# Tile 2's gate and value products as block products, with a new order of the steps around it

## The chip, the cores and the metric

The kernel runs on 1 core of a Trainium2 chip. Its engines are TensorE (PE), VectorE (DVE), ScalarE (ACT), GpSimd (POOL) and SyncE (SP), which here issues nearly all DMAs. The metric is the time of one execution in microseconds on the device; the median of several executions is what is compared.

## The reference

Causal attention with a window of 64 keys (8 batches, 8 heads, 576 positions, 64 per head), and behind it a gated layer on its 4608 tokens:

```python
scores = where(mask, q @ k.T / sqrt(64), -1e9)          # mask: 0 <= i - j < 64
x = softmax(scores) @ v                                 # 4608 tokens x 512
xn = x / sqrt(mean(x * x) + 1e-6) * rms_g
g = xn @ w_gate                                         # 512 x 1536
out = (g * sigmoid(g) * (xn @ w_val)) @ w_out           # 1536 x 512
```

All inputs and outputs are float32.

## The kernel before

The tokens are worked through in nine tiles of 512 (`t` = 0 to 8). The inner width of 1536 is cut into six chunks of 256 (`c`). For each tile the kernel first makes gate and value of all chunks ("gate and value stage"), then the product with `w_out` ("out stage"). Operands are split into a high and a low half in float16, and a product is the sum of three: high by high, high by low, low by high (`three`, L1534).

There are two ways for gate and value. Tiles 0 to `FIRST7` - 1 = 2 use `expert_in` (L1578): for each chunk and each half of it a product `pg` (gate) and one `pv` (value), each of 12 matmuls with 512 columns, in one of three PSUM banks of the pool `ps_mo`; ScalarE takes tanh of `pg` into `th`, VectorE multiplies `th` by `pg` and then by `pv`, and ScalarE and GpSimd split the result into the halves of `h`. Tiles from `FIRST7` on use `expert_in_7` (L1733): weights and tokens are cut into two by two blocks, and seven block products replace eight. A block product (`product`, L1717) has 12 matmuls with 256 columns, gate and value side by side in one bank `bk`. ScalarE copies three partial banks per chunk to SBUF (`s1`, `p5`, `u2`), VectorE adds them to the next ones, and the gates work on 256 columns at a time. Tiles from `FIRSTO` = 3 on also make their out stage by block products; tiles 0 to 2 use `expert_out` with the whole `h` (`chunk_out`).

The block products need seven left operands per chunk: three blocks of the weights and four sums of blocks. `prepare(c, step)` (L1628) makes them from the halves that lie in `wt0` to `wt11`: VectorE adds halves to whole blocks (`sum0`, `sum1`, `blk`), adds these, ScalarE casts to the high half of `hl`, VectorE subtracts for the low half, and SyncE writes both to DRAM (`sevens`). There are 50 such steps, `PREP` says between which points of time they fall. Time is counted in half steps, 32 to a tile: 24 in gate and value, 8 in out. `load_sevens` (L1705) later loads the operands, 256 KB each, into a ring of 15 places that are the high halves of `wt0` to `wt7`: so a place can be loaded when the last classic tile is through with that chunk's weights and `prepare` has read them.

The right operands of a tile in block form are made by `combine` (L1499): sums and differences of blocks of the tokens, split into halves. They lie in the tile's `xn`, in `wt18` or `wt19` by the parity of the tile (`operands`, L1489), and in `wt8` or, for the first such tile, in a small tile `t3`. Tile 1's first chunk of `h` lies in `wt18` (`HPLACE`, `h_tile`).

Between the products lies the attention of later batches, one visit for a pair of heads: TensorE makes scores and the product with the values; VectorE masks; ScalarE takes the exponential and scales; 13 copies of 32 rows exchange blocks of `pm` and VectorE turns them. `MOVE_ON` deals the copies out in turn: two for GpSimd, one for ScalarE.

Each engine works its instructions in order. That order is written out by hand: instructions are recorded, and the tables `ORDER` to `ORDER_3` say in which order they are emitted (a letter for the engine, the tile's name; `t` is the next TensorE step). `ORDER` holds all up to the end of tile 0's gate and value ("early list"); the others what follows.

The lines that matter most:

```python
FIRST7 = 3
PREP = ((27.5, 32, 9), (35, 88, 41))
for n, (c, p) in enumerate(SEVENS):
    x, y, w = banks[(c + parity(t)) % 2], banks[2], banks[5]
    acc = {1: x, 6: x, 7: x, 4: x, 2: y, 5: w, 3: w}[p]
    product(t, c, p, acc, p in (1, 2, 5))
```

Of the kernel before, what the change touches and what calls it, by code (L numbers as in the profile page):

```python
# [46 lines left out]
FIRST7 = 3  # L47
# [10 lines left out]
PREP = ((27.5, 32, 9), (35, 88, 41))  # L58
# [4 lines left out]
MOVE_ON = "gga"  # L63
SCALE = 0.5, 0.2
MOVE_BY = 0.8
# [126 lines left out]
t*39 s.pm_8 t*2 v.ssq_1 v.pm_8 s.pm_8 t v.ssq_1 t*2 s.pm_8 t*2 v.pm_8 t v.ssq_1 s.pm_8 t*4 v.pm_8 g.below t g.three_of  # L192
v.ssq_1 g.below t s.pm_8 v.pm_8 g.below*2 t v.ssq_1 g.below v.pm_8 g.below t s.pm_8 g.below v.ssq_1 t g.below v.pm_8
g.below t g.three_of v.ssq_1 g.three_of v.pm_8 s.pm_8 t g.three_of v.ssq_1 g.three_of t v.ssq_1 s.pm_8 t v.ssq_1 t
v.ssq_1 t s.pm_8 v.ssq_1 t*2 v.st_8 t v.ssq_1 t v.st_8 v.ssq_1 t s.pm_8*2 t s.pm_8 t s.pm_8 t s.pm_8 t s.pm_8 t s.pm_8
t s.pm_8 t s.pm_8 t*2 s.pm_8 g.pm_8 s.pm_8 g.pm_8*3
# [3 lines left out]
y.sevens3 v.sum1 y.sevens3 v.sum0 y.sevens3 v.sum1 v.blk_0_3 y.sevens3 v.sum1 y.sevens3 t*2 y.outs v.blk_0_3 t s.hl_0_2  # L200
t y.outs t s.pm_8 t y.outs s.pm_8 t*5 y.outs v.xb_1 t*2 y.outs g.pm_8 t v.xb_1 t s.xn_1 y.outs t*2 v.xb_1 y.sevens5
s.xn_1 t g.xn_1 t y.sevens0 t s.pm_8 v.xb_1 t s.xn_1 y.sevens5 t v.hl_0_2 t g.xn_1 y.sevens5 s.xn_1 t*2 y.sevens5
v.sum0 t*2 y.sevens5 t*3 y.sevens5 t g.xn_1 t y.sevens5 t v.xb_1 s.hl_0_4 t y.sevens0 v.xb_1 t v.xb_1 t s.xn_2
y.sevens5 v.xb_1 t s.xn_2 t s.xn_2 v.hl_0_4 g.xn_1 y.sevens5 t s.xn_2 t y.sevens5 v.sum1 t*3 y.sevens5 t*7 y.sevens0
# [307 lines left out]
def tile_window_attention_moe(  # L512
# [484 lines left out]
    def scores_of_pair(n, sc, first):  # L997
# [30 lines left out]
        for i, u in enumerate(order):  # L1028
            after(done + SCALE[0] + SCALE[1] * i, partial(even, u))

# [1134 lines left out]
```

## Time and profile before

| | us |
|---|---|
| median of 3 runs | 931.2 |
| lowest and highest | 930.34, 932.97 |
| the profiled execution | 933.73 |
| its span | 931.9 |

The span is what the hardware profiler saw of the profiled execution, from its first instruction to its last; its own time has 1.8 us more around it. In the views, `line` is that of a recording helper, so instructions are told apart by their tiles: `pg`, `pv`, `po` are banks of the classic products, `bk` banks of block products. The stages of this execution, by the first matmul of each: tile 0's out from 142.80 us, tile 1 from 175.93, its out from 249.71, tile 2 from 286.02, its out from 355.49, tile 3 from 390.94, its out from 452.3.

### The profile page before, as it was taken

How to read it: one execution, taken by the hardware profiler on the slowest of the kernel's cores; microseconds unless marked ns; L12 is line 12 of the kernel's file. 1: busy time of each engine (PE TensorE's matmuls, PEld its weight loads, DVE VectorE, ACT ScalarE, POOL GpSimd, SP SyncE). 2: the span in 40 equal slices, each digit the busy share in tenths (PEclk: the TensorE clock that was granted, in tenths of full speed). 3: DMA queues.
4: the chain of work that ended last, by engine and by line, in shares of the span. 5: the costliest groups of instructions: out<-in, count | busy, mean ns of one | idle time of the engine just before them, and what ended most of it. 6: DMA issues, size and time to landing. Idle time of an engine off the chain costs nothing.

```text
span 931.9 us, 23553 instructions
## 1 busy us (share of the span) xinstructions
PE 912.2 (98%) x8668; PEld 669.7 (72%) x8668; DVE 708.3 (76%) x1970; ACT 639.2 (69%) x1692; POOL 399.7 (43%) x555
## 2 busy tenths in 40 slices
PE   9799999999999999999999999999999999999998
PEld 6545544544444444588888888888888888888887
DVE  6799889676786898688868987888778767734760
ACT  7679987668646776599858886888598435623550
POOL 4355554545364563245444644455445322220330
PEclk9799999999999999999999999999999999999999
DMA  9775666653316744298868777777776667777613
GB/s 289 227 243 175 238 181 161 165 162 98 115 53 181 226 136 124 68 369 247 262 218 241 231 245 238 232 233 219 235 216 188 210 218 203 202 243 206 185 58 125
DMA packets 124772, 183.22 MB, mean 197 GB/s; under 512 B 30192, under 2 KB 59888, under 8 KB 124656
## 3 DMA queue, kind: packets, MB, share of 16 engines
q1 hardware_dynamic: 124080, 180.83, 64.0%
q8 instruction: 68, 1.11, 0.5%
q10 hardware_dynamic: 576, 0.88, 0.3%
q14 instruction: 48, 0.39, 0.1%
HBM read 155.72 MB, written 25.95 MB: 195 GB/s over the span
## 4 chain that ended last, share of the span: by engine, by line
PE 68%; DVE 12%; ACT 10%; DMA 5%; issue 3%; POOL 1%; SPq 1%; ACTq 0%; DVEq 0%; POOLq 0%
PE bk L574 48%; PE po L574 7%; ACT pm L574 6%; DMA kv<-kv 4%; PE pg L574 3%; PE xp L574 3%; DVE th L574 3%; PE pv L574 2%; PE sc L574 2%; DVE pm L574 2%; DVE sum L574 1%; POOL pm L574 1%; ACT th L574 1%; PE pw L574 1%; DVE hl L574 1%
## 5 line engine op out<-in xcount | busy, mean ns | idle before, releaser
L574 PEld LDWEIGHTS <-wt 128*128 128x128 f16 x3912 | 381.2, 98 | 140.6 <-issue 9.6
L574 PE MATMUL bk<-xn,wt 128*128 128x256 f16 x1728 | 208.3, 273 | 0.6 <-DMA wt<-sevens 0.4
L574 POOL TENSOR_TENSOR hw<-th,hw 128x256 f16<-128x256 f32 x72 | 68.0, 962 | 247.4 <-ACT hw L574 189.8
L574 PE MATMUL bk<-hw 128*128 128x256 f16 x1512 | 169.4, 273 | 0.6 <-ACT ot L574 0.6
L574 PEld LDWEIGHTS <-hw 128*128 128x128 f16 x1512 | 146.7, 98 | 18.7 <-issue 1.8
L574 ACT ACTIVATE pm<-pm,st 128x128 f32<-128x128 f32 (+1 forms) x432 | 149.3, 385 | 10.5 <-DVE st L574 10.3
L574 PE MATMUL bk<-wt,wt 128*128 128x256 f16 x1224 | 150.4, 273 | 2.0 <-ACT u L574 2.0
L574 POOL COPY pm<-pm 32x288 f32<-32x288 f32 (+1 forms) x218 | 107.3, 492 | 94.8 <-ACT pm L574 86.3
L574 PE MATMUL pg<-xn,wt 128*128 128x512 f16 x432 | 108.2, 380 | 0.4 <-DVE th L574 0.4
L574 PE MATMUL pv<-xn,wt 128*128 128x512 f16 x432 | 106.3, 380 | 1.0 <-DVE th L574 1.0
L574 PE MATMUL po<-wt,h 128*128 128x512 f16 x408 | 90.7, 379 | 0.0
L574 ACT ACTIVATE th<-bk,hsc 128x256 f32<-128x256 f32 x108 | 51.0, 472 | 37.9 <-PE bk L574 18.0
L574 PEld LDWEIGHTS <-h 128*128 128x128 f16 x408 | 39.2, 98 | 46.3 <-issue 0.5
L574 DVE SCALAR_TENSOR_TENSOR th<-th,bk 128x256 f32<-128x256 f32 x108 | 44.8, 415 | 27.5 <-ACT th L574 27.0
L574 POOL TENSOR_TENSOR xn<-xb,xn 128x448 f16<-128x448 f32 (+7 forms) x49 | 40.6, 848 | 40.3 <-ACT xn L574 39.8
L574 POOL TENSOR_TENSOR h<-th,h 128x512 f16<-128x512 f32 x30 | 38.7, 1292 | 39.8 <-ACT h L574 35.3
L574 DVE TENSOR_TENSOR bk<-bk,s 128x512 f32<-128x512 f32 x36 | 25.1, 697 | 31.9 <-PE bk L574 14.8
L574 PE MATMUL sc<-kv,q 64*64 64x128 f32 (+1 forms) x1056 | 47.7, 279 | 1.0 <-DVE ssq L574 0.7
L574 DVE SCALAR_TENSOR_TENSOR th<-bk,th 128x256 f32<-128x256 f32 x108 | 45.2, 418 | 2.1
L574 DVE STREAM_TRANSPOSE pm<-pm 128x512 f32<-128x512 f32 (+1 forms) x72 | 38.7, 556 | 10.1 <-POOL pm L574 9.8
L574 DVE CUSTOM_DVE_ANT_0 pm<-sc,blocked 128x128 f32<-128x128 f32 x192 | 44.2, 278 | 0.6 <-PE sc L574 0.6
L574 POOL TENSOR_TENSOR hw<-sb,hw 128x512 f16<-128x512 f32 x36 | 42.9, 1192 | 0.9 <-ACT hw L574 0.8
(184 smaller groups left out, 1495.1 us busy)
## 6 DMA issues: line engine op xcount, KB each, us to landing
wt<-sevens SPq DMA_DIRECT2D x252, 256.0 KB, 3.1
hw<-outs SPq DMA_DIRECT2D x84, 384.0 KB, 5.3
kv<-kv SPq DMA_DIRECT2D x28, 608.0 KB, 4.9
q<-q SPq DMA_DIRECT2D x29, 288.0 KB, 4.6
kv<-kv SPq DMA_DIRECT2D x65, 128.0 KB, 5.5
st<-w_gate SPq DMA_DIRECT2D x6, 1024.0 KB, 9.2
st<-w_val SPq DMA_DIRECT2D x6, 1024.0 KB, 6.8
st_o<-w_out SPq DMA_DIRECT2D x6, 1024.0 KB, 5.1
```

Source lines behind the costliest of these rows:

```text
L574: steps[next(tensor) if name == "t" else name].popleft()()
```

## The change

`FIRST7` becomes 2, so tile 2's gate and value are made by 42 block products; its out stage stays classic. All preparation of the blocks has to be made before it: the second stretch of `PREP` ends at 63 half steps, in tile 1's out stage, and not at 88. Tile 2's right operands now lie in `wt18`, so tile 1's first chunk of `h` lies in `wt19`. `MOVE_ON` deals the copies of a visit out one by one to GpSimd and ScalarE. `SCALE_ON` brings a way to scale weights on other engines, but "aaa" leaves all of it on ScalarE. `ORDER_0`, `ORDER_1` and `ORDER_3` are written anew; `ORDER` is the same.

```diff
-FIRST7 = 3
+FIRST7 = 2
...
-PREP = ((27.5, 32, 9), (35, 88, 41))
+PREP = ((27.5, 32, 9), (32.5, 63, 41))
...
-MOVE_ON = "gga"
+MOVE_ON = "ga"
 SCALE = 0.5, 0.2
+SCALE_ON = "aaa"
...
 ORDER_1 = """
-y.q_10 y.sevens0*12 y.sevens1*5 y.q_11 y.sevens1*7 y.sevens2 y.kv_10*3 y.sevens2*11 y.sevens4 y.sevens3*7 v.sum0
...
         for i, u in enumerate(order):
-            after(done + SCALE[0] + SCALE[1] * i, partial(even, u))
+            part = SCALE_ON[slot(u) // 4]
+            if part == "a":
+                after(done + SCALE[0] + SCALE[1] * i, partial(even, u))
+            elif u == 0:
+                after(done + SCALE[0], partial(even_first, engine_of(part)))
+            elif slot(u) % 4 == 0:
+                after(done + SCALE[0] + SCALE[1] * i, partial(even_four, engine_of(part), slot(u)))
...
-    HPLACE = "8fffff"
+    HPLACE = "9fffff"
```

`even_four` and `even_first`, which the diff also brings, are called for no letter of "aaa".

VectorE's order in tile 1's gate and value stage, from the last step on `th_1_2` on (first the tile, then the half of a chunk, 0 to 11). Before:

```order
L574 SCALAR_TENSOR_TENSOR th_1_2_2221<-pv_1_2_2222,th_1_2_2221 128x512
L574 TENSOR_TENSOR blk_2_3_2263<-wt4_91 128x256
L574 TENSOR_TENSOR blk_2_3_2263<-wt5_92 128x256
L574 TENSOR_TENSOR hl_1_7_2244<-sum1_2181,hl_1_7_2244 128x512
L574 SCALAR_TENSOR_TENSOR th_1_3_2225<-th_1_3_2225,pg_1_3_2224 128x512
L574 TENSOR_TENSOR sum1_2181<-wt4_91 128x256
L574 TENSOR_TENSOR sum1_2181<-wt5_92 128x256
L574 SCALAR_TENSOR_TENSOR th_1_3_2225<-pv_1_3_2227,th_1_3_2225 128x512
L574 TENSOR_TENSOR sum1_2181<-sum1_2181,sum0_2180 128x512
L574 STREAM_TRANSPOSE pm_10_2215<-pm_10_2215 128x512 x2
L574 STREAM_TRANSPOSE pm_10_2215<-pm_10_2215 64x128
L574 SCALAR_TENSOR_TENSOR sum0_2180<-sum0_2180,blk_2_3_2263 128x512
```

In the change, the same place:

```order
L588 SCALAR_TENSOR_TENSOR th_1_2_2227<-pv_1_2_2229,th_1_2_2227 128x512
L588 TENSOR_SCALAR st_10_2221<-st_10_2221 128x9
L588 TENSOR_TENSOR hl_1_7_2228<-sum1_2181,hl_1_7_2228 128x512
L588 RECIPROCAL st_10_2221<-st_10_2221 128x9
L588 TENSOR_TENSOR sum1_2181<-wt4_91 128x256
L588 TENSOR_TENSOR sum1_2181<-wt5_92 128x256
L588 SCALAR_TENSOR_TENSOR th_1_3_2231<-th_1_3_2231,pg_1_3_2230 128x512
L588 TENSOR_TENSOR sum1_2181<-sum1_2181,sum0_2180 128x512
L588 SCALAR_TENSOR_TENSOR th_1_3_2231<-pv_1_3_2232,th_1_3_2231 128x512
L588 SCALAR_TENSOR_TENSOR sum0_2180<-sum0_2180,blk_2_3_2238 128x512
L588 TENSOR_TENSOR hl_2_2_2233<-sum1_2181,hl_2_2_2233 128x512
L588 TENSOR_TENSOR sum1_2181<-sum1_2181,blk_2_3_2238 128x512
```

Where before one split (`hl_1_7`) and one step of chunk 2 stood among these `th` steps, now two splits (`hl_1_7`, `hl_2_2`) stand there, and a visit's turn (`STREAM_TRANSPOSE`) has moved behind.

VectorE's order at the start of tile 2, before:

```order
L574 SCALAR_TENSOR_TENSOR th_2_0_2320<-th_2_0_2320,pg_2_0_2319 128x512
L574 TENSOR_TENSOR blk_4_3_2325<-wt8_95 128x256
L574 TENSOR_TENSOR blk_4_3_2325<-wt9_96 128x256
L574 SCALAR_TENSOR_TENSOR sum0_2180<-sum0_2180,blk_4_3_2325 128x512
L574 SCALAR_TENSOR_TENSOR th_2_0_2320<-pv_2_0_2321,th_2_0_2320 128x512
L574 TENSOR_TENSOR sum1_2181<-sum1_2181,blk_4_3_2325 128x512
L574 TENSOR_TENSOR hl_4_4_2332<-sum0_2180,hl_4_4_2332 128x512
L574 TENSOR_TENSOR hl_4_5_2336<-sum1_2181,hl_4_5_2336 128x512
```

In the change:

```order
L588 TENSOR_TENSOR bk2_3794<-bk2_3794,s1_3802 128x512
L588 TENSOR_TENSOR wsum_1_0_3810<-wsum_1_1_3813,wsum_1_0_3810 128x256
L588 SCALAR_TENSOR_TENSOR th_2_0_0_3807<-th_2_0_0_3807,bk2_3794 128x256
L588 TENSOR_TENSOR wsum_1_1_3813<-wsum_1_1_3813,wsum_1_0_3810 128x256
L588 SCALAR_TENSOR_TENSOR th_2_0_0_3807<-bk2_3794,th_2_0_0_3807 128x256
L588 TENSOR_TENSOR bk5_3798<-bk5_3798,u2_3803 128x512
L588 TENSOR_TENSOR wsum_1_1_3813<-wsum_1_1_3813 128x256
L588 TENSOR_SCALAR st_14_2327<-st_14_2327 128x9
L588 RECIPROCAL st_14_2327<-st_14_2327 128x9
L588 TENSOR_TENSOR whl_0_5_3812<-wsum_0_1_2328,whl_0_5_3812 128x512
L588 SCALAR_TENSOR_TENSOR th_2_0_0_3807<-th_2_0_0_3807,bk5_3798 128x256
L588 SCALAR_TENSOR_TENSOR th_2_0_0_3807<-bk5_3798,th_2_0_0_3807 128x256
```

The blocks and splits of chunk 4 are gone; whole-bank adds into `bk2` and `bk5` and `th` steps of 256 columns have come.

SyncE's queue in the first half of tile 1's gate and value stage (`wt0<-sevens` is a ring load, `sevens<-hl` a write of the preparation, `kv` and `q` feed visits). Before:

```order
L574 DMA sevens1_129<-hl_1_4_2226 128x2x256 x2
L574 DMA kv_11_2206<-kv 128x1216
L574 DMA sevens1_129<-hl_1_5_2232 128x2x256 x2
L574 DMA kv_11_2206<-kv 64x512 x2
L574 DMA q_13_2261<-q 128x576
L574 DMA sevens1_129<-hl_1_7_2244 128x2x256 x2
L574 DMA q_14_2286<-q 128x576
L574 DMA kv_12_2231<-kv 128x1216
L574 DMA kv_12_2231<-kv 64x512 x2
L574 DMA sevens2_130<-hl_2_2_2258 128x2x256 x2
```

In the change:

```order
L588 DMA sevens1_129<-hl_1_4_2212 128x2x256
L588 DMA wt0_87<-sevens0_128 128x1024 x2
L588 DMA kv_11_2209<-kv 128x1216
L588 DMA kv_11_2209<-kv 64x512 x2
L588 DMA q_13_2271<-q 128x576
L588 DMA sevens1_129<-hl_1_5_2223 128x2x256
L588 DMA wt1_88<-sevens0_128 128x1024 x2
L588 DMA sevens1_129<-hl_1_5_2223 128x2x256
L588 DMA sevens1_129<-hl_1_7_2228 128x2x256 x2
L588 DMA wt2_89<-sevens0_128 128x1024
L588 DMA wt2_89<-sevens1_129 128x1024
L588 DMA wt3_90<-sevens0_128 128x1024
```

The loads of the ring, which before stood in tile 2, now stand between the writes of `hl`.

## Rows read from the trace of the kernel before

**Rows 1.** The page, part 1 and span: engine, busy us, share of the span, instructions.

```profile
span 931.9 us, 23553 instructions
...
PE 912.2 (98%) x8668; PEld 669.7 (72%) x8668; DVE 708.3 (76%) x1970; ACT 639.2 (69%) x1692; POOL 399.7 (43%) x555
```

**Rows 2.** Table by stage: length, busy us of each engine, granted clock, DMA share, GB/s.

```profile
48.00:142.80 94.80, 92.72 (x684) 48.49 (x683) 85.55 (x222) 82.89 (x161) 50.22 (x62) 0.99 0.67 210
...
175.93:249.71 73.78, 72.44 (x578) 36.21 (x576) 50.73 (x137) 50.64 (x149) 34.83 (x51) 1.00 0.45 127
249.71:286.02 36.31, 34.44 (x254) 16.56 (x253) 27.78 (x88) 21.04 (x67) 14.25 (x20) 1.00 0.36 107
286.02:355.49 69.47, 69.47 (x505) 34.17 (x504) 58.80 (x127) 48.54 (x133) 41.71 (x48) 1.00 0.60 176
...
390.94:452.30 61.36, 61.26 (x709) 54.12 (x707) 48.98 (x139) 57.10 (x165) 31.54 (x44) 1.00 0.90 287
```

**Rows 3.** TensorE in order of time, tiles 2 and 3: start, length, what.

```profile
309.18 2.75 PE L574 MATMUL pg<-xn,wt 128*128 128x512 f16 x12
...
324.72 2.75 PE L574 MATMUL pg<-xn,wt 128*128 128x512 f16 x12
...
390.94 1.47 PE L574 MATMUL bk<-xn,wt 128*128 128x256 f16 x12
...
394.87 1.47 PE L574 MATMUL bk<-wt,wt 128*128 128x256 f16 x12
```

**Rows 4.** The same view, rows with a wait: in brackets idle time and releaser.

```profile
194.49 2.75 PE L574 MATMUL pg<-xn,wt 128*128 128x512 f16 x12 [0.35 <-DVE th L574]
...
265.19 0.34 PE L574 MATMUL rb<-ssq,three_of 128*128 128x144 bf16 x3 [1.87 <-DVE ssq L574]
...
543.48 1.47 PE L574 MATMUL bk<-wt,wt 128*128 128x256 f16 x12 [0.99 <-ACT u L574]
...
638.35 1.47 PE L574 MATMUL bk<-wt,wt 128*128 128x256 f16 x12 [0.99 <-ACT u L574]
```

**Rows 5.** The page, part 5: the weight loads.

```profile
L574 PEld LDWEIGHTS <-wt 128*128 128x128 f16 x3912 | 381.2, 98 | 140.6 <-issue 9.6
```

**Rows 6.** ScalarE, groups by form, 286.02 to 452.3 us: count, busy, mean ns, idle before.

```profile
L574 ACT ACTIVATE th<-pg,hsc 128x512 f32<-128x512 f32 x12 | 8.2, 679 | 1.6 <-DVE sum L574 0.8 <-PE pg L574 0.8
L574 ACT ACTIVATE th<-bk,hsc 128x256 f32<-128x256 f32 x17 | 8.0, 470 | 1.1 <-DVE bk L574 0.8
...
L574 ACT CAST hl<-sum 128x512 f16<-128x512 f32 x7 | 4.3, 621 | 1.0 <-DMA sevens<-hl 0.9
...
L574 ACT COPY s<-bk 128x512 f32<-128x512 f32 x6 | 3.5, 583 | 0.1
```

**Rows 7.** VectorE, groups by form, tile 1, 175.93 to 249.71 us.

```profile
L574 DVE TENSOR_TENSOR hl<-sum,hl 128x512 f16<-128x512 f32 x11 | 8.9, 806 | 9.4 <-ACT hl L574 9.3
...
L574 DVE TENSOR_TENSOR sum<-wt 128x256 f32<-128x256 f16 x10 | 5.5, 577 | 0.0
...
L574 DVE TENSOR_TENSOR blk<-wt 128x256 f32<-128x256 f16 x10 | 4.4, 462 | 0.0
L574 DVE TENSOR_TENSOR sum<-sum,blk 128x512 f32<-128x512 f32 x5 | 3.4, 689 | 0.1
```

**Rows 8.** DMA issues: count, KB each, median us to landing.

```profile
wt<-sevens SPq DMA_DIRECT2D x252, 256.0 KB, 3.1
...
sevens<-hl SPq DMA_DIRECT2D x48, 128.0 KB, 2.0
```

**Rows 9.** Instructions on the tiles blk, whole span: ns min/median/max, first and last start.

```profile
L574 DVE TENSOR_TENSOR blk<-wt x24: 372/418/1371, 155.4 to 332.6; 128x256 f32<-128x256 f16 x24
```

**Rows 10.** ScalarE in order of time, start of tile 1.

```profile
184.11 0.69 ACT L574 ACTIVATE th<-pg,hsc 128x512 f32<-128x512 f32 x1 [3.74 <-DMA sevens<-hl]
```

**Rows 11.** ScalarE, groups by form, whole span: its copies between turns.

```profile
L574 ACT COPY pm<-pm 32x288 f32<-32x288 f32 x48 | 20.6, 430 | 1.0
...
L574 ACT COPY pm<-pm 32x256 f32<-32x256 f32 x49 | 19.7, 401 | 0.8
```

More of the change, by code (lines that the diff above doesn't have):

```diff
@@ L191 @@
 ORDER_0 = """
[L192 to L196, printed above, removed]
+t*39 s.pm_8 t*2 v.ssq_1 v.pm_8 s.pm_8 t v.ssq_1 t*2 s.pm_8 t*2 v.pm_8 t v.ssq_1 s.pm_8 t*4 v.pm_8 g.below t v.ssq_1
@@ L197 @@
+g.below t v.pm_8 s.pm_8 g.below*2 v.ssq_1 t g.below v.pm_8 g.below t g.below s.pm_8 v.ssq_1 g.below v.pm_8 t g.below
+g.three_of v.ssq_1 t v.pm_8 s.pm_8 g.three_of t g.three_of v.ssq_1 g.three_of t g.three_of v.ssq_1 s.pm_8 t v.ssq_1 t
+v.ssq_1 s.pm_8 t v.ssq_1 t*2 v.st_8 t v.ssq_1 v.st_8 t v.ssq_1 t s.pm_8 t s.pm_8 t s.pm_8 t s.pm_8 t*2 s.pm_8 t s.pm_8
+t s.pm_8 t*2 s.pm_8*3 g.pm_8 s.pm_8 g.pm_8 s.pm_8 g.pm_8
 """
 ORDER_1 = """
-y.q_10 y.sevens0*12 y.sevens1*5 y.q_11 y.sevens1*7 y.sevens2 y.kv_10*3 y.sevens2*11 y.sevens4 y.sevens3*7 v.sum0
@@ L200 @@
[L200 to L204, printed above, removed]
@@ L503 @@
[L503 to L507 removed]
+y.q_10 y.sevens0*12 y.sevens1*5 y.q_11 y.sevens1*7 y.sevens2 y.kv_10*3 y.sevens2*11 y.sevens3*8 v.sum0 y.sevens3 v.sum0
@@ new lines @@
+s.ssq_3 t*8 s.ot_1_3 y.
+"""
+ORDER_2 = """
+g.pm_10 g.wsum_1_0 v.pm_10*2 v.pm_11*8 t*2 v.pm_10 t*2 v.wsum_0_0 t*3 v.wsum_1_0 t s.pm_11 t*2 v.wsum_0_0 t*2 s.pm_11 t
+y.kv_15 t v.wsum_0_1 t*2 s.s1 t y.q_15 t v.wsum_0_1 t*3 s.whl_0_4 y.wt0 t*5 s.wt7 t v.whl_0_4 y.wt0 t*4 y.q_16 s.pm_11
+t*2 g.wsum_1_1 t*2 y.kv_15 s.pm_11 t*3 v.bk2 t y.wt1 t s.pm_11 t*3 y.kv_15 t s.pm_11 v.wsum_1_0 t*3 y.q_17 t s.th_2_0_0
+t*3 y.wt1 t s.u2 t v.th_2_0_0 t*2 y.outs t v.wsum_1_1 s.pm_11 t*3 y.outs v.th_2_0_0 t*2 s.pm_11 t v.bk5 t y.wt2 t*2
@@ new lines @@
+t g.xn_3 v.whl_5_5 t*2 s.xn_3 t y. t s.wt8 t g.xn_3 t v.xb_3 t y.outs t*2 y.outs g.wt8 t*2 s.wt19 t*2 v.wt19 t g.pm_11
+t*2 v.xb_3 t*3 s.wt19 v.xb_3 t*2 s.xn_3 t*4 v.xb_3 t*2 v.xb_3 t*2 v.xb_3 s.xn_4 t v.xb_3 t g.xn_4 t v.wt19 s.xn_4 t*2
+s.xn_4 t g.xn_4 t v.xn_3 t s.ot_2_2 t*2 g.xn_4 t v.t3_4_320 t y. t*2 y. t s.wt8 v.xb_3 t*2 s.wt18 g.wt8 t*2 v.wt18 t*3
+v.xb_3 t*3 s.wt18 v.xb_3 t*2 v.wt18 s.xn_4 t*2 v.xn_4 t*26 s.xb_4 t v.pm_9 t*4 s.xb_4 t*7 s.ssq_4 t*12 s.ot_2_3 y.
+"""
+ORDER_3 = """
+g.pm_11 v.pm_11*3 v.pm_9*8 v.hsc t*8 s.pm_9 t*4 s.pm_9 t y.kv_19 t*3 s.s1 t y.q_19 t*4 s.pm_9 y.wt6 t*5 s.wt7 t y.wt6
@@ L508 @@
+s.hw t*2 v.hw t*3 s.hw t*2 g.hw t*2 y.hw t*9 g.hw t*8 s.wt7 t y.hw t*4 y.hw t*4 y.hw t*27 s.u2 t*36 v.ot_8_3 t*7 y. t*4
+y. t*25 v.ot_8_4 t*7 y. t*4 y. t*25 v.ot_8_5 t*7 y. t*4 y. t*5 s.ot_8_6 t y. t*17 s.ot_8_6 y.
 """
```

611 lines of the change are left out of this document (310 added, 301 removed).

## Prediction

> **What bounds the kernel now.** I read the engine shares first: TensorE is busy for 98% of the span, VectorE for 76% and ScalarE for 69% [rows 1]. A busy TensorE only bounds a stage if nothing interrupts it, so I read next the table by stage. From 286.02 to 355.49 us (tile 2, gate and value) it shows 69.47 busy in 69.47 us, all at the full granted clock, the 2.4 GHz level [rows 2]. Tile 2 is purely bound by TensorE: shortening its matmuls shortens the kernel, as long as the engines that feed it keep up. Third, I read TensorE in order of time, to price its units [rows 3], and the few waits that the same view shows [rows 4]. In tile 1 (175.93 to 249.71) it idles 73.78 - 72.44 = 1.34 us, as at 194.49 until a VectorE `th` step [rows 2, 4]; in tile 2 never; in tile 3, the first one in block form, 0.1 us.
>
> A time forecast here is for the median. The profiled execution took 933.73 us for its span of 931.9; the median of the three runs is 931.2, so 2.5 us lower. I apply the difference worked out on that execution to the median. About 0.3%, 2.8 us, is what a measurement of this kernel can tell from no change: faster means under 928.4, slower over 934.0.
>
> **The products of tile 2.** Removed: 24 products (6 chunks, 2 halves, gate and value) of 12 matmuls of 512 columns. Six of them in a row start within 324.72 - 309.18 = 15.54 us, so one takes 2.59: 62.2 us. Added: 42 block products (6 chunks, 7 each) of 12 matmuls of 256 columns. Three of those in tile 3 start within 394.87 - 390.94 = 3.93 us, so one takes 1.31: 55.0 us [rows 3]. The attention work between them is the same. Difference **-7.1 us**, all on the path today.
>
> A shorter matmul need not be proportionally cheaper, since each still has its weight load of 98 ns [rows 5]. The rows say it is: 109 ns (1.31 us by 12) against 216 ns, though the weight loads fill 54.12 of tile 3's 61.36 us and only 34.17 of tile 2's 69.47 [rows 2, 3]. The Trainium skill, "TensorE: Matmul & The Clock Gate", section on the back-to-back issue gap, speaks against this change: in streams with weight loads it puts a matmul of 512 columns at about 131 ns and one of 128 at about 81; between them, an estimate from that page, 98 ns for 256. By it, 288 x 131 = 37.7 us would become 504 x 98 = 49.4, a loss of 11.7 us, 942.9. The trace has 216 and 109 ns for the same things and so speaks against the rule; what it leaves of it is rival 4.
>
> **What tile 2's engines get.** Six chunks bring 18 copies of a bank to SBUF on ScalarE, 18 x 0.585 = 10.5 us, and 23 half-width tanh in place of 12 whole ones, 23 x 0.47 - 12 x 0.68 = 2.7; seven `hl` casts leave, 7 x 0.62 = 4.3 [rows 6]. ScalarE goes from 48.5 to about 57.4 us of a stage of 69.5 - 7.1 = 62.4. VectorE gains 18 whole-bank adds, 18 x 0.69 = 12.4 us by the price of a sum of that size, and loses 26 preparation adds and splits, 12 to 21 us at 0.46 to 0.81 apiece [rows 7]; twice as many `th` steps of half the width change little. It stays about or under its 58.8. Tile 3 already runs with ScalarE at 57.10 of 61.36 us and TensorE idle for 0.1 [rows 2]. DMA: 27 ring loads of 256 KB more and 14 writes of 128 KB fewer than the 176 GB/s x 69.47 us = 12.2 MB of before make 12.2 + 7.1 - 1.8 = 17.5 MB in 62.4 us, 280 GB/s, where tile 3 moved 287 with next to no stall [rows 2, 8]. Cost taken: +0.2 us. Bounds: 0, and some 2 us, two stalls such as the 0.99 us at 543.48, until ScalarE had copied a bank [rows 4].
>
> **The preparation, now all before tile 2.** The weight blocks were made by 41 steps spread over tiles 1 and 2; now they must end inside tile 1. By the order, VectorE gets in tile 1's gate and value stage 6 more adds of halves (0.577), 5 more sums (0.69), 4 more blocks (0.462) and 5 more splits (0.806): 3.5 + 3.4 + 1.8 + 4.0 = 12.7 us [rows 7]. The small operand sums of tile 2 come in and a visit's turns go out, about 0.5 more. VectorE rises from 50.73 to some 64 of 73.78 us; ScalarE gets 5 casts and two `pm` copies more, 4 us, and some steps of visits, 50.64 to under 60 of 73.78 [rows 2, 6, 11]. Neither is full, but each works in order, and VectorE idles now for 23 us mostly because it waits: for `hl` casts alone 9.3 us [rows 7]. What stands behind a `th` step is TensorE, which has three banks for these products: at 194.49 it waited 0.35 us until VectorE had freed one [rows 4]. With 64 instead of 51 us of work on VectorE there will be more such waits.
>
> Nothing in the trace has this stage at this load. The nearest rows: tile 0 (48 to 142.8) had VectorE busy 85.55 of 94.8 us and TensorE idle 2.1; tile 2 had 58.80 of 69.47 and none [rows 2]. Lower bound: below nothing, -1.3, since the new order may also remove the present waits. Upper bound: VectorE keeps all its 73.78 - 50.73 = 23 us of waits, and the stage grows by 64 + 23 - 73.8 = 13.2. I take as much again as today's idle time, **+1.4 us**, because the rows at 85 to 90% load lie at 0 to 2.1.
>
> What the added adds cost is itself uncertain: one of 128x256 took 0.372 to 1.371 us, median 0.418 [rows 9]. The Trainium skill, "GPSIMD Engine Reference", key points, names a reason: GpSimd shares its SBUF interfaces with VectorE's instructions of two SBUF inputs. The order takes 15 of the 36 `pm` copies off GpSimd in this stage. By that rule the additions come nearer to their lower prices (four blocks and six half adds at 0.418 in place of 0.46 to 0.58, an estimate: 1.1 us less on VectorE), which would lead towards rival 1; no row here parts the two engines' times.
>
> **SyncE's queue.** 15 ring loads move into tile 1's stage, and each waits for the products of the chunk whose weights it overwrites; the block writes behind it wait too, and with them the buffers that ScalarE's next `hl` or `th` wants. Such a wait stands at 184.11: 3.74 us of ScalarE until a write to `sevens` had landed [rows 10]. It is part of the 1.4. The loads themselves have tile 1's out stage (36.31 us, DMA share 0.36) to land, at 3.1 us each [rows 2, 8]: nothing; if that cover were gone, one landing, 3.1 us. The chunk of h in another buffer: nothing, the same writes and reads in SBUF.
>
> **Later tiles.** Every second `pm` copy goes to ScalarE instead of every third: 28 more after tile 2, 28 x 0.415 = 11.6 us [rows 11], by the order some 1.5 us of it in the gate and value stage of each of tiles 3 to 5, where ScalarE has 61.36 - 57.10 = 4.3 us left [rows 2]; the rest lies in out stages. Two stalls of 0.99 us end there with a ScalarE copy, at 543.48 and 638.35 [rows 4]. Taken: +0.6. Bounds: -2 (both vanish) and +3 (each of three tiles gets one more).
>
> **Sum**: -7.1 + 0.2 + 1.4 + 0.6 = -4.9, so 931.2 - 4.9 = **926.3 us**.
>
> **Rivals.**
> 1. *Nothing new waits.* All 7.1 us stay: 924.1; if the new order also removes the stalls of tile 1 and of the later tiles (1.3 + 2.0) and part of the 1.87 us before tile 1's `rb` [rows 4], down to about 919. For it: tile 3 runs the block form with ScalarE at 93% and no stall. Against: VectorE's waits in tile 1. Chance 0.20.
> 2. *ScalarE becomes the bound of the block tiles.* Tile 2 and tiles 3 to 5 stall two or three times 0.99 us each, 4 to 6 us in all: 929 to 931. For it: the stalls at 543 and 638 already end with ScalarE's snapshot. Against: out stages give it room to catch up, as tile 1's, where it is busy 21.04 of 36.31 us [rows 2]. Chance 0.14.
> 3. *VectorE becomes the bound of tile 1.* If its 23 us of waits stay and some 13 us of work are added, the stage grows by up to 13.2 us: 931.2 - 7.1 + 13.2 = 937.3, slower than before. It decides against the change once the stage grows by over 7.1, that is when more than 73.8 + 7.1 - 64 = 16.9 of the 23 us stay. For it: its waits are for ScalarE's casts, which also become more. Against: tile 0 ran VectorE at 90%. Chance 0.07.
> 4. *The block matmuls are not cheaper*, because a quarter of each 98 ns weight load shows: 504 x (109 + 25) ns = 67.5 us in place of 62.2, +5.3: 936.5. It turns the sign from 62.2 / 504 = 123 ns a matmul on. Tile 3's 109 ns nearly exclude it. Chance 0.01.
> 5. *The change doesn't do what it says.* The order holds 504 matmuls of 256 columns for tile 2, so only its gain could be hidden: TensorE isn't the bound of tile 2. With 69.47 of 69.47 us busy: 0.02, 931.2.
>
> **How the numbers follow.** Forecast with its band 924.1 to 928.4: 0.56. Faster: 0.56 + 0.20 = 0.76 less a little for its edge, 0.75. Same: rival 2, rival 5 and the edge, 0.17. Slower: rivals 3 and 4, 0.08. The range leaves out half of rival 1 and rival 3: 922.6 to 931.0.
>
> **What would show it.** Tile 2's gate and value stage near 62.5 us with products 1.31 apart; tile 1's near 75.2 with VectorE near 64 busy, and waits only on `th`. Wrong if tile 1's stage takes over 78 us, if tile 2's shows TensorE waits on ScalarE's `s`, `u` or `wt` copies above 1 us in sum, or if stages 3 to 5 grow.

## The result, and the profile after the change

The changed kernel takes **922.2 us** (median of 4 runs, 918.58 to 924.62) against 932.09 for the kernel before in the same series: a ratio of 0.9887 [0.9839, 0.9935], 9.9 us less. A second series (5 runs, the experiment `after_again`) gave 921.07 us and 0.9883 [0.9862, 0.9905]. Forecast were 926.3 us, 922.6 to 931.0. The sign was right; the gain is twice as large as forecast and lies just outside the range.

The profiled execution took 918.58 us for a span of 916.8. The engine shares of its page answer to [rows 1]: TensorE is still the busy one, VectorE and ScalarE have a little more to do and GpSimd less.

```profile
span 916.8 us, 24156 instructions
...
PE 899.9 (98%) x8873; PEld 688.8 (75%) x8884; DVE 719.3 (78%) x2026; ACT 673.0 (73%) x1777; POOL 376.1 (41%) x506
```

The table by stage of the changed kernel answers to [rows 2], with the same columns (stretch, length, busy us of each engine with its instructions, granted clock, DMA share, GB/s). The lines are tile 1's gate and value, its out stage, tile 2's gate and value, tile 3's.

```profile
173.46:247.43 73.97, 72.23 (x578) 36.19 (x577) 63.45 (x163) 57.41 (x170) 28.20 (x37) 1.00 0.63 189
247.43:281.84 34.41, 34.41 (x254) 16.55 (x253) 30.43 (x81) 24.08 (x69) 19.93 (x26) 1.00 0.30 91
281.84:345.01 63.17, 62.63 (x716) 54.72 (x714) 53.82 (x157) 57.06 (x165) 29.57 (x33) 1.00 0.93 291
379.30:440.31 61.01, 61.01 (x709) 54.11 (x708) 49.39 (x139) 58.06 (x168) 28.95 (x38) 1.00 0.89 288
```

Tile 2 went from 69.47 to 63.17 us, with ScalarE at 57.06 where 57.4 was forecast and the DMAs at 291 GB/s where 280 was. TensorE in order of time, at the start of tile 2 (start, length, what), shows why: the products are 1.31 us apart, as in tile 3 before [rows 3].

```profile
281.84 1.47 PE L588 MATMUL bk<-xn,wt 128*128 128x256 f16 x12
283.15 1.47 PE L588 MATMUL bk<-wt,wt 128*128 128x256 f16 x12
284.46 1.47 PE L588 MATMUL bk<-xn,wt 128*128 128x256 f16 x12
```

But that is not all that moved. The waits of TensorE from tile 1 to the end, summed by releaser (total, times, longest), answer to [rows 4]: neither the wait of `rb` on `ssq` nor those on `u` are there any more. (The `ssq` steps are VectorE's chain of short steps for the inverse root of the mean square of the next tokens; TensorE spreads its result with `rb`. This is called the root chain below. `u` is ScalarE's copy of a partial bank, `ot` a part of the output, `hw` and `whl` are split operands of block products.)

```profile
PE pg L588 <- DVE th L588: 1.6, 1, 1.6
PE bk L588 <- ACT ot L588: 0.6, 1, 0.6
PE bk L588 <- DVE th L588: 0.5, 1, 0.5
PE pv L588 <- DVE th L588: 0.2, 1, 0.2
```

Up to the end of tile 0's gate and value (`ORDER`) every kernel here has the same list of steps, yet the length of this part varies from profile to profile. Tile 0's out stage takes 33.1 us in all of them, so tile 1 begins between 170.26 and 176.89 us. So stages are compared from tile 1's first product on. All profiles of this study, worked out from TensorE in order of time (us; the last two columns are sums):

| kernel | tile 1 | out 1 | tile 2 and out 2 | tile 3 to end | from tile 1 to end |
|---|---|---|---|---|---|
| before | 73.78 | 36.31 | 104.92 | 540.96 | 755.97 |
| after | 73.97 | 34.41 | 97.46 | 537.50 | 743.34 |
| after_again (the same kernel) | 76.94 | 34.38 | 98.07 | 537.42 | 746.81 |
| before_ga | 74.58 | 34.60 | 104.90 | 543.44 | 757.52 |
| before_chain | 73.82 | 34.27 | 103.75 | 541.09 | 752.93 |
| after_gga | 78.49 | 34.28 | 98.02 | 537.98 | 748.77 |
| after_old_late | 78.24 | 34.38 | 97.91 | 543.74 | 754.27 |
| before_sp | 71.90 | 34.47 | 106.29 | 540.91 | 753.57 |
| after_sp | 71.90 | 34.28 | 97.78 | 537.50 | 741.46 |
| before_sp_chain | 71.90 | 34.28 | 103.75 | 540.48 | 750.41 |
| after_sp_load | 77.80 | 39.08 | 97.19 | 537.47 | 751.54 |
| after_sp_load2 | 71.90 | 36.77 | 97.14 | 537.50 | 743.31 |

In three of these profiles TensorE's granted clock is below 1.00 in tile 1 itself: 0.96 in `after_gga`, 0.98 in `after_old_late` and in `after_sp_load`. In all the others it is 1.00 there.

From before to after that is -12.6 us with the first profile and -9.2 with the second, around the 9.9 of the runs. About 7 us of it are in tile 2 with its out stage, as forecast; 1.9 lie in tile 1's out stage and 3.5 behind tile 3, where the forecast had +0.6. Tile 1 takes 0.2 or 3.2 us more, depending on the profile.

### The profile page after: what moved, and what is told of

Read it like the earlier page. It is cut to its first block, busy times and chain, and to the rows that moved or that the text cites. A ratio compares the mean times of both kernels' runs of the same rounds, so it can differ in the third digit from the quotient of the medians.

```text
span 916.8 us, 24156 instructions
## 1 busy us (share of the span) xinstructions
PE 899.9 (98%) x8873; PEld 688.8 (75%) x8884; DVE 719.3 (78%) x2026; ACT 673.0 (73%) x1777; POOL 376.1 (41%) x506
## 3 DMA queue, kind: packets, MB, share of 16 engines
q8 instruction: 69, 1.13, 0.5%
## 4 chain that ended last, share of the span: by engine, by line
PE 85%; DMA 5%; DVE 4%; ACT 3%; issue 1%; SPq 1%; ACTq 0%; DVEq 0%
PE bk L588 61%; PE po L588 7%; PE pv L588 5%; PE pg L588 4%; PE xp L588 4%; DMA kv<-kv 4%; PE sc L588 3%; ACT pm L588 1%; DVE wt L588 1%; DVE th L588 1%; DMA st<-w_val 1%; DMA sevens<-hl 1%; SPq L588 1%; ACT th L588 0%; PE tot L588 0%
## 5 line engine op out<-in xcount | busy, mean ns | idle before, releaser
L588 PEld LDWEIGHTS <-wt 128*128 128x128 f16 x4128 | 402.1, 98 | 110.6 <-issue 6.1
L588 PE MATMUL bk<-xn,wt 128*128 128x256 f16 x2016 | 242.5, 273 | 0.6 <-DVE th L588 0.5
L588 PE MATMUL bk<-wt,wt 128*128 128x256 f16 x1440 | 176.9, 273 | 0.0
L588 POOL COPY pm<-pm 32x288 f32<-32x288 f32 (+1 forms) x169 | 84.4, 499 | 77.5 <-ACT pm L588 71.1
L588 ACT ACTIVATE th<-bk,hsc 128x256 f32<-128x256 f32 x126 | 59.5, 473 | 32.9 <-DVE bk L588 16.6
L588 DVE SCALAR_TENSOR_TENSOR th<-th,bk 128x256 f32<-128x256 f32 x126 | 52.5, 417 | 31.5 <-ACT th L588 31.0
L588 PE MATMUL pg<-xn,wt 128*128 128x512 f16 x288 | 74.8, 379 | 1.8 <-DVE th L588 1.6
L588 PE MATMUL pv<-xn,wt 128*128 128x512 f16 x288 | 73.0, 379 | 0.2 <-DVE th L588 0.2
L588 ACT COPY pm<-pm 32x288 f32<-32x288 f32 (+1 forms) x146 | 60.7, 416 | 2.6
L588 PE MATMUL po<-wt,h 128*128 128x512 f16 x264 | 59.0, 379 | 0.0
```

Of the source, the lines that this page charges most:

```text
L588: steps[next(tensor) if name == "t" else name].popleft()()
```

## The experiments

Two questions were open. What took the old waits away: the new **order** of the steps, or the new **dealing** of the `pm` copies (`MOVE_ON`)? And what makes tile 1 vary between 74 and 78 us with the same steps: VectorE's load, as the forecast had it, or something else?

### before_ga: the dealing alone

```diff
-MOVE_ON = "gga"
+MOVE_ON = "ga"
```

In the tables of the order, 147 entries change their letter from `g.pm_*` to `s.pm_*` or back, at the places where they stand.

> The kernel before with the change's dealing of the pm copies alone (every second one to ScalarE, MOVE_ON "ga"), at the places where its own order has them. Theory 'order' (the waits of tile 1's out stage, of tile 2's and of the late tiles went because steps were put in another order): little is gained. GpSimd has 7 copies in place of 9 ahead of the turn that holds the root chain in tile 1's out stage, 2 x 0.448 = 0.9 us, so the rb wait falls from 1.87 to about 1.0; the rb wait of tile 2's out stage (0.99) stays; the two u waits of tiles 4 and 5 (0.99 each) stay or grow to 1.4 to 1.8, as ScalarE has two copies more near them. Sum -0.9 to +1: 931 to 933, not to be told from before. Rival 'dealing' (the 28 copies that leave GpSimd freed the turns, whatever the order): all four waits go, -4.8 us: about 927.

Measured: 933.16 us, ratio 1.0009 [0.9993, 1.0024], no gain. TensorE's waits from tile 1's out stage to the end:

```profile
PE bk L571 <- ACT u L571: 3.2, 3, 1.3
PE bk L571 <- DVE th L571: 1.7, 3, 0.8
PE rb L571 <- DVE ssq L571: 1.0, 1, 1.0
```

The late waits on `u` stay and a third one joins them (1.33 us in tile 3), with some on `th`: behind tile 3 this kernel is 2.5 us longer than before. One thing came out differently: the 1.87 us of tile 1's out stage went entirely, where I expected 1.0 to stay. By the stages this kernel is 1.6 us longer from tile 1 on; by the runs there is no difference.

### before_chain: the order alone, at four places

In tile 1's out stage (`ORDER_1`) the two turns of `pm_10` go behind the root chain; the same is done with the last `whl` step and two of its writes in tile 2's out stage, and with four `s.pm` copies ahead of `s.u2` in the last chunk of tiles 4 and 5 (`ORDER_3`).

```diff
-v.ssq_2 v.pm_10 t*3 v.ssq_2 t v.pm_10 t*3 v.ssq_2 v.blk_3_6 t*2 v.ssq_2 t v.blk_3_6 t v.ssq_2
+v.ssq_2 t*3 v.ssq_2 t*4 v.ssq_2 v.blk_3_6 t*2 v.ssq_2 t v.blk_3_6 t v.ssq_2 v.pm_10*2
...
-s.pm_9*3 s.th_4_4_1 s.hw s.pm_9 s.u2
+s.th_4_4_1 s.hw s.u2 s.pm_9*4
```

(The second pair of lines names ScalarE's steps of tile 4 only.)

> The kernel before with four places of its order changed and nothing else: in tile 1's out stage the two turns behind the root chain's ssq steps; in tile 2's out stage the whl step and its two writes behind that chain; in the last chunk of tiles 4 and 5 four pm copies of ScalarE behind the copy to u. The dealing stays 'gga'. Theory 'order': the waits 1.87, 0.99, 0.99 and 0.99 go, -4.8 us: out stage of tile 1 34.4 in place of 36.31, tile 2 with its out stage 103.9 in place of 104.92, from tile 3's first product to the end 539 in place of 540.96; time 927 to 928. Rival 'dealing', or that other steps wait at the same places: less than 1.5 us gained, over 930.

Measured: 927.18 us, ratio 0.9953 [0.9937, 0.9968]. The waits aimed at are gone, and others are there, from tile 1's out stage to the end:

```profile
PE rb L571 <- DVE ssq L571: 0.9, 2, 0.5
PE bk L571 <- ACT ot L571: 0.6, 1, 0.6
PE bk L571 <- DVE hw L571: 0.3, 1, 0.3
```

The out stages of tiles 1 and 2 gave 2.0 and 1.2 us, as expected. Behind tile 3 nothing was won (541.09 against 540.96): TensorE waits instead for the root chains of the out stages of tiles 4 and 5 (2 x 0.47). In tile 4's, two short steps of the chain take 0.98 and 1.11 us, where they took 0.18 each before, while GpSimd works on `hw` (547.49 to 549.78). That the copies put behind `u` bring this about is not shown. The time came out as expected, but by the stages the four edits are worth 755.97 - 752.93 = 3.0 us, at the edge of what the runs allow (-5.9 to -3.0).

### after_gga and after_old_late: undoing one thing of the change

`after_gga` is the changed kernel with the old dealing at the new places. `after_old_late` is the changed kernel with the old order (`ORDER_3`) from tile 3 on, dealt as the changed kernel does.

```diff
-MOVE_ON = "ga"
+MOVE_ON = "gga"
```

> The changed kernel with the dealing of before (every third pm copy to ScalarE, MOVE_ON "gga") at the places of its own order. Theory 'order': no rb wait over 0.9 and no u wait comes back, as the turn and the root chain stay where the new order has them: 922 to 923.5. Rival 'dealing': the waits of before come back, about +4.8: 927.

Measured: 923.82 us, ratio to before 0.991 [0.9887, 0.9932]. Nothing of the old waits came back: from tile 1's out stage to the end TensorE waits 0.8 us on `th` in all, beside 0.6 on `ot` at the very end, which every version has.

In `after_old_late`, `ORDER_3` is that of the kernel before, with the letters of "ga" and the changed kernel's sequence of ring loads.

> The changed kernel with the order of the kernel before for everything from tile 3 on (dealing 'ga', at the places of that order). Everything up to tile 2's out stage is the changed kernel's. Theory 'order': the waits on u in tiles 4 and 5 come back, 0.99 each or more as ScalarE has more copies ahead of u; from tile 3's first product to the end 540 to 541 in place of 537.5, the time 924.5 to 926. Rival 'dealing': 537.5 as in the changed kernel, 922.

Measured: 930.72 us, ratio to before 0.9983 [0.9963, 1.0002]: with the old order behind tile 3 nearly nothing is left of the gain. The waits from there on:

```profile
PE bk L585 <- ACT u L585: 3.2, 3, 1.3
PE bk L585 <- DVE th L585: 1.7, 3, 0.8
```

They are the same, line for line, as in `before_ga`. So the order is the cause of the late gain: old order with old dealing 540.96 us, with new dealing 543.44 and 543.74, new order with either dealing 537.50 and 537.98. Under the new dealing the late order is worth 6.2 us, where I had expected 3, and the time of 924.5 to 926 was missed. What else lies between this kernel and the changed one is tile 1, 78.24 us in this profile, although its steps there are the changed kernel's own.

### after_again: the changed kernel once more

> The changed kernel as it is, once more. In its first profile tile 1's gate and value stage took 73.97 us, with a TensorE wait of 1.58 on th; in the two experiments that share its tile 1 (after_gga, after_old_late) 78.49 and 78.24, with one wait of 3.79 and 4.06 at the second value product. Theory 'SyncE' (the stage is set by how far SyncE's queue, which issues one write of about 0.5 us after the other from 127 us on, lies behind TensorE when the stage begins): this run shows one of the two pictures, with the wait the longer the later kv is issued before the burst of writes (147.27 in the first profile, 149.87 and 150.52 in the two others); the median of the times lies at 922 to 924, some runs at 918 to 920. Rival 'those experiments' orders did it': 74 us and 918 to 920 in nearly all runs.

Measured: 921.07 us (919.28 to 925.53), in the profile a tile 1 of 76.94 us with three waits on `th` for `pv` (2.3 us) and one for `pg` (2.2). The queue of SyncE shows what stands ahead of them. In order of time (start, length, what, count), first the changed kernel, where tile 1 begins at 173.46:

```profile
148.87 18.31 SPq L588 DMA_DIRECT2D sevens<-wt  x34
167.28 0.41 SPq L588 DMA_DIRECT2D sevens<-hl  x1
167.74 1.00 SPq L588 DMA_DIRECT2D sevens<-wt  x2
168.84 0.41 SPq L588 DMA_DIRECT2D sevens<-hl  x1
169.29 4.58 SPq L588 DMA_DIRECT2D sevens<-wt  x9
173.98 0.41 SPq L588 DMA_DIRECT2D sevens<-hl  x1
```

Then `after_again`, where it begins at 176.89:

```profile
152.92 19.07 SPq L588 DMA_DIRECT2D sevens<-wt  x34
172.09 0.41 SPq L588 DMA_DIRECT2D sevens<-hl  x1
172.55 1.01 SPq L588 DMA_DIRECT2D sevens<-wt  x2
173.65 0.41 SPq L588 DMA_DIRECT2D sevens<-hl  x1
174.11 4.58 SPq L588 DMA_DIRECT2D sevens<-wt  x9
178.79 0.41 SPq L588 DMA_DIRECT2D sevens<-hl  x1
```

The raw weight blocks (`sevens<-wt`) are issued back to back, some 0.5 us each (4.58 us for nine), and the write of an `hl` that is ready stands behind them: in `after_again` VectorE has made its split at 174.69, and the next write of an `hl` is issued at 178.79. `blk`, `hl`, `th` and `ot` share a pool of eight buffers (`t2k`), so VectorE and ScalarE then wait until a buffer is written out; in the changed kernel's first profile they do so for 4.72 and 4.20 us, in `after_again` for 6.06 and 5.56, and everything behind them, `th` included, comes late:

```profile
183.10 0.76 DVE L588 TENSOR_TENSOR blk<-wt 128x256 f32<-128x256 f16 x2 [6.06 <-DMA sevens<-hl]
184.34 0.62 ACT L588 CAST hl<-sum 128x512 f16<-128x512 f32 x1 [5.56 <-DMA sevens<-hl]
186.86 0.69 ACT L588 ACTIVATE th<-pg,hsc 128x512 f32<-128x512 f32 x1 [1.89 <-DMA out<-ot]
```

The stage is the longer the farther the queue is behind TensorE, though not in strict order. The write behind the nine is issued 0.52 us after tile 1's first product in the profile with 73.97 us, 1.90 after it in that with 76.94, and 2.88 and 3.02 after it in those with 78.49 and 78.24 (`after_gga`, `after_old_late`); TensorE's waits on `th` in the stage are 1.7, 4.5, 3.8 and 4.5 us. It is not, as I had written, the time at which `kv` is issued (latest in `after_again`, 151.32).

The two longest stages hold something else as well. During their waits of 3.79 and 4.06 us TensorE's granted clock fell, to 0.53 from 186.8 to 194.0 us in `after_gga` and to 0.54 from 188.6 to 192.3 in `after_old_late`, close to the level of 1.2 GHz. The product behind the wait then took 5.28 and 4.21 us, where 2.75 is usual. In `after_gga` (the stretch with the columns of the table by stage, then TensorE):

```profile
186.80:194.00 7.20, 5.72 (x14) 2.01 (x14) 6.42 (x16) 7.07 (x20) 2.60 (x5) 0.53 0.58 178
```

```profile
188.28 5.28 PE L586 MATMUL pv<-xn,wt 128*128 128x512 f16 x12 [3.79 <-DVE th L586]
```

So the queue's lag stands behind the waits, and some 2.8 and 1.5 us of these two stages are slower products at the lower clock.

### after_sp: 24 writes of the queue later

In `ORDER_1`, 12 entries `y.sevens4` and 12 `y.sevens5` leave their places ahead of tile 1 and stand in the middle of tile 1, in two groups of 12, one entry per three matmuls.

> The changed kernel with 24 writes of SyncE's queue moved and nothing else: the raw weight blocks of chunks 4 and 5 (12 writes to sevens4, 12 to sevens5), which its order issues before tile 1, come in the middle of tile 1, where the queue is idle. 24 x 0.51 = 12 us of issue leave the stretch before tile 1's second chunk. Theory 'SyncE': the writes of hl and ot are issued as soon as they are ready, VectorE's and ScalarE's waits of 4 to 7 us on sevens<-hl and out<-ot go, and with them the stall on th: tile 1 in 72.4 to 73.2 us in place of 74 to 78.5, the time 917 to 920. Rival 'VectorE' (64 us of work on VectorE make the stall): tile 1 stays at 74 to 78.5 and the time at 922 to 924. Rival 'moved wait': the writes in mid tile hold up ring loads or hl writes there, and as much is lost as won.

Measured: **916.67 us** (914.87 to 919.96), ratio to before 0.9841 [0.9815, 0.9867]; the changed kernel in the same series took 921.07. In this profile TensorE does not wait once in tile 1. The stage is 71.90 us long and wholly busy, although VectorE has 65.69 us of work in it:

```profile
176.74:248.64 71.90, 71.90 (x577) 36.24 (x576) 65.69 (x171) 59.66 (x176) 28.64 (x37) 1.00 0.66 191
```

And the queue is through with its raw blocks before tile 1 begins:

```profile
164.67 0.98 SPq L586 DMA_DIRECT2D sevens<-wt  x2
165.75 2.48 SPq L586 DMA_DIRECT2D sevens<-hl  x3
168.32 0.42 SPq L586 DMA_DIRECT2D q<-q  x1
168.83 1.50 SPq L586 DMA_DIRECT2D sevens<-hl  x3
```

This version beats both kernels. The stage was held up by SyncE's issues, not by VectorE's load. Slow transfers are not the reason either: from 165 to 190 us a write of an `hl` took a median of 2.3 us from issue to landing in the changed kernel's first profile and 2.5 in `after_again`, but 2.9 here, where nothing stalls.

### before_sp: the same edit in the kernel before

The same entries of `ORDER_1` move in the same way.

> The kernel before with the same 24 writes (sevens4, sevens5) of SyncE's queue moved to the middle of tile 1, and nothing else. Theory 'SyncE': the queue's lag is older than the change; in the profile of before it shows as ScalarE's 3.74 us on sevens<-hl and as TensorE's 1.34 us of waits on th in tile 1. Those waits go: tile 1 in 72.4 to 72.8 in place of 73.8, about -1.2 us, the time near 930.8. Rival 'only the change has it' (its preparation and VectorE's 64 us): tile 1 stays at 73.8 and the time at 932.

Measured: 930.8 us, ratio 0.997 [0.9944, 0.9997]. Tile 1 falls to 71.90 us as well, VectorE busy 52.58 of them, so the lag is older than the change. The 1.9 us of tile 1 and the wait in its out stage are won, but the wait on `ssq` in tile 2's out stage grows from 0.99 to 2.05 and gives back 1.1 (1.4 by the stages).

### after_sp_load and after_sp_load2: more work for VectorE

```diff
     whole_block(kept_block["b"], f, d)
+    if c in (1, 3, 5):
+        whole_block(kept_block["b"], f, d)
```

> after_sp with more work on VectorE: the half-width additions of the weight blocks of chunks 1, 3 and 5 are done twice (12 more of some 0.46 us, 5 us in all, nearly all in tile 1; the second writes the same numbers over the first). VectorE goes from 65.69 to about 70.5 of tile 1's 71.90 us. Theory 'VectorE is a bound only when its work fills the stage': tile 1 stays at 72 to 73.5. Rival 'VectorE's waits stay whatever its load' (rival 3 of the prediction): tile 1 grows by all the work added, to 76 or 77.

Measured: 923.62 us (one run), tile 1 in 77.80. This answers nothing about the load: VectorE waited 7.2 us in one piece for a ring load of weights, since the repeated additions stood apart from the first ones.

```profile
DVE blk L586 <- DMA wt<-sevens: 7.2, 1, 7.2
```

In the second version each addition is repeated in place, with its entry in the order doubled:

```diff
-    nc.vector.tensor_tensor(out[:, i], hi, lo, ALU.add)
+    for _ in range(2 if out is not s0 and out is not s1 and c in (1, 3, 5) else 1):
+        nc.vector.tensor_tensor(out[:, i], hi, lo, ALU.add)
```

> The same 12 additions as in after_sp_load, but each right behind the one that it repeats, so that none stands behind a ring load of its weights (there the second round waited 7.20 us for a wt<-sevens load, and some of the numbers were taken from weights already replaced). VectorE about 70.5 of 71.90 us in tile 1. Theory 'VectorE is a bound only when its work fills the stage': tile 1 in 71.9 to 73.5. Rival 'VectorE's waits stay whatever its load': 76 or 77.

Measured: 918.05 us (one run). Tile 1's gate and value stage and its out stage:

```profile
172.99:244.89 71.90, 71.90 (x577) 36.17 (x576) 66.93 (x172) 57.99 (x172) 28.66 (x37) 1.00 0.66 187
244.89:281.66 36.77, 34.45 (x254) 16.53 (x253) 32.17 (x84) 23.91 (x69) 20.24 (x26) 1.00 0.27 83
```

With VectorE at 93% tile 1 still does not stall. The load rose less than planned, from 65.69 to 66.93 us and not to 70.5. The additions repeated for chunks 1 and 3 made those in tile 1 3.7 us longer, but its count of VectorE's instructions rose only from 171 to 172: some 2.5 us of other work moved out of the stage. The additions of chunk 5 do not stand in tile 1 at all but in its out stage, ahead of the root chain and in the middle of it; there they take 2.7 us more, and `rb` waits 2.32 us. So this run tests a load of 93%, not of 98%.

### before_sp_chain: all order edits, without the block products

> The kernel before, tile 2 still with products of 512 columns, with both edits of its order: the moves of before_chain and the 24 writes of before_sp. So nearly all waits that the change's order removes are gone, and the one that it brought is too. Theory: the order is worth some -5 to -7 us on its own (before_chain measured -4.9, before_sp -2.0), so 925 to 927; what then still lies between this kernel and after_sp (916.67) is the block products of tile 2, 7.1 us, and the late waits that before_chain only moved (0.9 + 1.2 us in the out stages of tiles 4 and 5): 8 to 10 us. Rival 'the two edits remove the same waits': no better than before_chain alone, 927 to 928.

Measured: 927.39 us (921.2 to 928.61), ratio 0.9938 [0.9915, 0.996]: the interval spans -7.9 to -3.7 us, so the runs alone hardly tell it from `before_chain`. By the stages the edits do add up, 750.41 us from tile 1 on against 755.97, 752.93 and 753.57. Against `after_sp` (741.46) 8.95 us remain: 5.97 in tile 2 with its out stage, where `after_sp` waits 0.75 on `th`, and 2.98 behind tile 3.

## Why the prediction was right and wrong

**The products: right.** Forecast were 62.2 - 55.0 = 7.1 us. Tile 2 with its out stage went from 104.92 to 97.46 and 98.07; with the new waits on `th` in it (0.49 and 1.13) and the lost `rb` wait (0.99) put back, the products alone gave 7.46 + 0.49 - 0.99 = 6.96 and 6.85 + 1.13 - 0.99 = 6.99. A matmul of 256 columns took 109 ns here too. The Trainium skill, "TensorE: Matmul & The Clock Gate", section on the back-to-back issue gap, would by the estimate from its figures have had a loss of 11.7 us; this trace does not agree with it, as the rows before did not. Rival 4 is out.

**Tile 2's engines: right within the bounds.** +0.2 was taken, bounds 0 to 2; the waits are 0.49 and 1.13, on `th` and not, as the bound assumed, on a copy of ScalarE. Rival 2 (ScalarE as the bound) did not come either: in tile 3 ScalarE is busy for 58.06 of 61.01 us and TensorE for all of it.

**Tile 1: wrong in its cause, near in size by luck.** +1.4 was taken for VectorE's waits. VectorE came to 63.45 us (64 forecast) and ScalarE to 57.41 (under 60). The stage grew by 0.19 in one profile of the changed kernel and by 3.16 in the other. But the sentence "with 64 instead of 51 us of work on VectorE there will be more such waits" does not hold: with 65.69 us and the queue relieved there are none. The paragraph on SyncE's queue named the right wait, 3.74 us of ScalarE until a write had landed [rows 10], and then priced it within VectorE's term. It looked at the 15 ring loads that move into tile 1 and counted no issue time for the raw blocks ahead of it. Rival 3 rested on the same picture and fell with it.

The Trainium skill, "GPSIMD Engine Reference", key points, let me expect cheaper additions with fewer copies on GpSimd. As a whole they did not get cheaper: the median of the 24 additions to `blk` is 418 ns after as before [rows 9], and in tile 1 their mean rose from 462 to 563 ns [rows 7]. Yet the trace agrees with the page: what an addition costs depends on what GpSimd does beside it. In the changed kernel two additions to `blk` on VectorE, and what GpSimd does beside the first; beside the second it does nothing:

```profile
215.58 1.38 DVE L588 TENSOR_TENSOR blk<-wt 128x256 f32<-128x256 f16 x1
...
218.15 0.41 DVE L588 TENSOR_TENSOR blk<-wt 128x256 f32<-128x256 f16 x1
```

```profile
215.12 1.55 POOL L588 TENSOR_TENSOR h<-th,h 128x512 f16<-128x512 f32 x1 [2.24 <-ACT h L588]
```

Of the additions of weight halves to `blk` and `sum` in this profile, those with no GpSimd work beside them have a median of 0.41 us, the eight beside a copy 0.61, the seven beside a two-input operation 1.38. In tile 1 those beside copies fell from eight to five, but those beside GpSimd's splits of `h` rose from one to five. The forecast counted the copies and not the dearer neighbour.

**Waits elsewhere: this step failed.** The sum had +0.6 for later tiles, with bounds of -2 and +3, and nothing for the waits in the out stages of tiles 1 (at 265.19) and 2; that the waits at 265.19, 543.48 and 638.35 [rows 4] might go stood only in a bound and in rival 1. The prediction read the order for what the change adds, mainly ScalarE's 28 copies, and priced those as added waits. What happened is -3.5 behind tile 3, outside the bounds, -1.9 in tile 1's out stage and -1.0 for `rb` in tile 2's, 6.4 us in all. Of the 3.5, 2.0 are the two waits on `u` and 0.4 two waits for ring loads; the other 1.1 is no wait that a row names (TensorE is busy 533.44 us there in place of 534.61, with the same 5693 matmuls), and its cause stays open. `after_old_late` and `after_gga` show that the late part comes from the order of the steps and is there with either dealing. In ScalarE's order of time before, four `pm` copies lie ahead of the copy to `u` in the last chunk of tile 4:

```profile
540.10 1.29 ACT L574 COPY pm<-pm 32x288 f32<-32x288 f32 x3
...
542.42 0.40 ACT L574 COPY pm<-pm 32x256 f32<-32x256 f32 x1
542.84 0.59 ACT L574 COPY u<-bk 128x512 f32<-128x512 f32 x1
```

At the same place in the changed kernel there are three ahead of it, one stands behind, and TensorE does not wait:

```profile
526.71 0.87 ACT L588 COPY pm<-pm 32x288 f32<-32x288 f32 x2
...
528.61 0.43 ACT L588 COPY pm<-pm 32x288 f32<-32x288 f32 x1
529.07 0.59 ACT L588 COPY u<-bk 128x512 f32<-128x512 f32 x1
...
530.63 0.40 ACT L588 COPY pm<-pm 32x256 f32<-32x256 f32 x1
```

The direction of the dealing was judged rightly: with the old order it costs 2.5 us late (`before_ga`). Rival 1 had "if the new order also removes the stalls" with 919 as its end; it held the mechanism and got 0.20.

The wait of 1.87 in tile 1's out stage went by each of three separate means (dealing, order of the chain, the 24 moved writes), so which of them did it in the changed kernel is not settled. In the kernel before it was a root chain behind a turn that waited for GpSimd's copies:

```profile
262.55 0.71 DVE L574 STREAM_TRANSPOSE pm<-pm 128x512 f32<-128x512 f32 x1 [3.14 <-POOL pm L574]
```

## What to carry to other kernels

- When an order is made anew, look at every wait of the trace before and read in the new order what now stands ahead of its releaser; a wait that nobody meant to touch can be worth as much as the change itself. Here 6.4 us went that way beside 7.0 for the products.
- The queue that issues DMAs is an engine with its own time: some 0.5 us an issue, in order. Count what it has to issue ahead of a stage, and put writes that nobody needs soon behind those whose buffers are wanted. Moving 24 of them was worth 4.4 us in the changed kernel, by the medians.
- An in-order engine at 90% load need not stall anything: here VectorE at 91 and 93% of tile 1 held up nothing. It stalls what hangs on a chain in its queue: 2.7 us of additions that stood ahead of the root chain and in the middle of it cost TensorE 2.3 us.
- Look at the granted clock of a stage before its length is read as the cost of its waits: in three profiles (`after_gga`, `after_old_late`, `after_sp_load`) the clock fell to near half during a wait of 3.79, 4.06 and 4.30 us, and in the first two the next product took 5.28 and 4.21 us in place of 2.75. Whether the wait set this off was not tried.

## What the runs showed of the hardware

Up to tile 0's out stage all these kernels have the same list of steps, and the length of this part still differed by 6.6 us (137.16 to 143.78). It goes with TensorE's granted clock. The mean from the span's start to tile 0's out stage was 0.99 or 1.00 in the three profiles in which tile 1 begins first (170.26, 171.17 and 172.99 us: `after_sp_load`, `before_chain`, `after_sp_load2`), 0.98 in the next (after, 173.46), and 0.95 or 0.96 in the other eight (173.98 to 176.89). Most of the falls lie between 25 and 50 us, where the mean was 1.00 in `before_chain` and 0.73 in before, `after_again` and `after_sp`; `before_sp` and `before_sp_chain` fell once more, after 100 us (0.92 and 0.94 from 125 us to tile 0's out stage). Within the eight the clock does not set the order. The rows of the stretch from 25 to 50 us for `after_again` and for `before_chain` (columns as in the table by stage):

```profile
25.00:50.00 25.00, 20.57 (x233) 14.02 (x233) 19.84 (x67) 17.89 (x41) 12.35 (x15) 0.73 0.66 216
```

```profile
25.00:50.00 25.00, 20.07 (x265) 12.47 (x262) 22.54 (x75) 20.05 (x44) 14.88 (x17) 1.00 0.78 261
```

TensorE is about equally busy in both, but gets 233 matmuls done in one and 265 in the other. At 0.73 it spent about half of the 25 us at the lower level of 1.2 GHz; in the 25 us ahead, at the full level in both, it was busy for 21.9 us in `after_again` and for 21.5 in `before_chain`, where the clock did not fall. What sets the fall off was not tried. It is there in kernels with the change and without it, and it is why one profile's span should not be set against another's: the span of `after_sp` (918.2 us) is longer than that of the first profile of the changed kernel (916.8), while its median is 4 us lower.
